# The first pass's down stage of a fused attention and gated-FFN block: one of seven products taken to a second level

## The chip, the cores and the metric

The kernel runs on one core of a Trainium2 chip. The metric is the device time of one execution in microseconds. Before the change the median of three runs is 753.28 us (752.81 to 753.76).

## What is computed

With 2048 tokens, D = 1024, 32 heads of 32 and F = 3584, all in bf16:

```
xn  = layernorm(x)
s   = linear_attention(xn, wqkv) @ wo        # phi(q) (phi(k)^T v) / (phi(q) sum phi(k))
ffn = (silu(xn @ w_gate) * (xn @ w_up)) @ w_down
out = x + s * silu(ffn)
```

The change concerns the last product, `@ w_down`, for the second half of the tokens, with the outer `silu`, the product with `s` and the addition of `x` that finish each result.

## The kernel before

The first 243 us or so make `s` and write it to DRAM (`s_dram`). What follows goes in two passes over 1024 tokens each; the one over tokens 1024 to 2047 comes first. A pass has 28 units (gate and up for 14 groups of 256 hidden columns) that fill `h`, and then the down stage, which multiplies `h` (1024 x 3584) with `w_down` (3584 x 1024). The first pass's down stage is `emit_down` (L1229), the last pass's `emit_down_m` (L1417).

All these products use a scheme with seven products in place of eight (Strassen's, in Winograd's form): both operands are cut in 2 x 2, seven products M1 to M7 of sums of the quarters are taken, and the four quarters of the result are C11 = M1 + M2, C12 = M1 + M6 + M5 + M3, C21 = M1 + M6 + M7 + M4 and C22 = M1 + M6 + M7 + M5. In the down stage the quarters of `h` are token halves of 512 by even and odd chunks of 128 hidden columns, those of `w_down` the matching rows by halves of 512 columns. The sums of weights are made once and kept in DRAM as tiles of two kinds: an "a" tile holds the weights of M1, M5, M6 and M7 for two steps of k, a "b" tile those of M2, M3 and M4 (seven tiles each).

`emit_down` works on four token tiles t = 0 to 3 of 128, each with 14 steps of k:

- **The a phase** (L1354): tiles 0 and 1, then 2 and 3, the second of each pair 6 steps behind (`LEAD`). `step_a` (L1253) issues four products of 512 columns per step: M1 into bank `dx`, M6 into `dy`, M7 and M5 into the double bank `dzw`. `evac_a` (L1281) copies M1 on ACT, adds on DVE, finishes C22's SiLU on ACT and keeps M1 and the sums.
- **The b phase** (L1382): first tiles 2 and 3, whose banks still hold M7, M5 and M1, then tiles 0 and 1 in fresh banks. `step_b` (L1272) issues three products of 512 columns: M2, M4 and M3. `evac_b` (L1303) adds what was kept (DVE) and takes the SiLUs (ACT).
- **Finishing a result** is `fin` (L1219): two DVE operations (times `s`, plus `x`), the output DMA on POOL's queue, and `io_load`, which loads the next `x` and `s` pair on SP's queue into one of five buffers, in the order of the list `fq`. A load waits until the output that last used its buffer has landed. The last three results of the pass are finished in the first three units of the next pass (`deferred`).
- **Work for the last pass**, which takes M1, M2, M4 and M7 each by seven products of a second level: `l2_early` (L1119) makes the second-level weight sums of M2 in free room of each b tile, four POOL operations per tile (L1137), and later stores them by three DMAs on SP (L1129 to L1131).
- **Sums for the next pass** (`emit_Ssum`, L706): four DVE operations of 128x2048, here between the two phases.

The orders of PE, DVE, ACT and POOL are the program's. SP's queue, which carries loads and stores, is ordered by a scheduler within `emit_down`; in most other parts by hand. Weight tiles rotate through eight slots: a b tile waits until the a tile in its slot has been read for the last time, and the next pass's tiles wait for the b tiles.

The second level in the last pass is `l2_M` (L1487). M is itself cut in 2 x 2 (256 tokens, 256 columns) and done by products 1, 2, 5, 6, 7, 4, 3, each two row tiles of seven matmuls of 256 columns (`l2_p`, L1473). Products share four banks: ACT copies half of a bank into another where two results share a sum (L1496, L1504), and between products 7 and 4 the banks are partly emptied by DVE while PE does other products (`fill`).

Of the kernel before, what the change touches and what calls it, by code (L numbers as in the profile page):

```python
# [21 lines left out]
def kernel(  # L22
# [11 lines left out]
    nc = tc.nc  # L34
# [919 lines left out]
    with ExitStack() as p3:  # L954
# [274 lines left out]
        def emit_down(p, h, base, last, more_S, next_S):  # L1229
# [13 lines left out]

            def alloc(t, phase):
                x_ = pps.tile([P, CW], FP32, name="dx", tag="s")
                y_ = pps.tile([P, CW], FP32, name="dy", tag="s") if phase == "a" else None
                zw = ppd.tile([P, 2, CW], FP32, name="dzw", tag="d")
                bk[t] = (x_, y_, zw)
# [3 lines left out]

            def step_a(t, k):  # L1253
                if k == 0:
                    alloc(t, "a")
# [8 lines left out]
            def prods_b(t, k, fresh):  # L1264
                x_, y_, zw = bk[t]
# [6 lines left out]
            def step_b(t, k, fresh):  # L1272
                if k == 0 and fresh:
                    alloc(t, "b")
                for f in prods_b(t, k, fresh):
                    f()

            fin_e = (nc.vector, nc.vector, nc.sync if last else nc.gpsimd)
            pend = []

            def evac_a(t, keep):  # L1281
# [5 lines left out]
                else:  # L1287
                    s1 = k2([P, CW], FP32, "s1")[:]
# [3 lines left out]
                nc.vector.tensor_tensor(out=s2, in0=y_[:], in1=s1, op=ALU.add)  # L1292
                nc.vector.tensor_tensor(out=s3, in0=zw[:, 0, :], in1=s2, op=ALU.add)
                c22 = k2([P, CW], FP32, "c22")[:] if keep else s3
                if keep:
                    nc.vector.tensor_tensor(out=u4, in0=zw[:, 1, :], in1=s2, op=ALU.add)
                nc.vector.tensor_tensor(out=c22, in0=zw[:, 1, :], in1=s3, op=ALU.add)
                g_ = k2([P, CW], BF16, "g22")[:]
                nc.scalar.activation(out=g_, in_=c22, func=ACT.Silu, scale=rch)
                pend.append(lambda: fin(p, t + TPB, 1, g_, *fin_e))  # L1300
                kept[t] = (s1, st[:, 1:3, :]) if keep else s2

            def evac_b(t, fresh):  # L1303
                x_, _, zw = bk[t]
                d = m4.tile([P, 2, CW], FP32, name="dd", tag="m4")
                g_ = k2([P, 2, CW], BF16, "g12")
                g11 = k2([P, CW], BF16, "g11")[:]
                if fresh:
                    s1, s34 = kept[t]
                    c11 = k2([P, CW], FP32, "c11")[:]  # L1310
                    nc.vector.tensor_tensor(out=d[:], in0=zw[:], in1=s34, op=ALU.add)
                    nc.vector.tensor_tensor(out=c11, in0=x_[:], in1=s1, op=ALU.add)
                    nc.scalar.activation(out=g_[:], in_=d[:], func=ACT.Silu, scale=rch)
                    nc.scalar.activation(out=g11, in_=c11, func=ACT.Silu, scale=rch)
                else:
                    s2 = kept[t]
                    nc.vector.tensor_tensor(out=d[:], in0=zw[:], in1=s2[:, None, :].to_broadcast([P, 2, CW]),
                                            op=ALU.add)
                    nc.scalar.activation(out=g11, in_=x_[:], func=ACT.Silu, scale=rch)
                    nc.scalar.activation(out=g_[:], in_=d[:], func=ACT.Silu, scale=rch)  # L1320
                return [lambda: fin(p, t + TPB, 0, g_[:, 0, :], *fin_e),
                        lambda: fin(p, t, 1, g_[:, 1, :], *fin_e),
                        lambda: fin(p, t, 0, g11, *fin_e)]

            def finish(t):
                ps = [ppd.tile([P, 2, CW], FP32, name="dz", tag="d")[:, 0, :]]
                ps += [pps.tile([P, CW], FP32, name="df%d" % i, tag="s")[:] for i in range(3)]
                s1, s34 = kept[t]
                t1, t2 = slice(t * P, (t + 1) * P), slice(TB + t * P, TB + (t + 1) * P)
                hs_ = [slice(0, 3 * CW // 4), slice(3 * CW // 4, CW)]  # L1330
                for i in range(2):
                    nc.scalar.copy(out=ps[2 + i][:, 0:hs_[i].stop - hs_[i].start], in_=s1[:, hs_[i]])
                for q, (r0, cc) in enumerate(((t + TPB, 0), (t, 1))):
                    for k in range(NFG):
                        lhs = h[:, 2 * k, t2].bitcast(F16) if q else h[:, 2 * k + 1, t2]
                        mm(ps[q], lhs, wb(k, 2 - q), k == 0, k == NFG - 1)
                    d = k2([P, CW], FP32, "d%d" % q)[:]
                    g_ = k2([P, CW], BF16, "g%d" % q)[:]
                    nc.vector.tensor_tensor(out=d, in0=ps[q], in1=s34[:, q, :], op=ALU.add)
                    nc.scalar.activation(out=g_, in_=d, func=ACT.Silu, scale=rch)  # L1340
                    if q == 0:
                        f0 = (r0, cc, g_)
                fin(p, *f0, *fin_e)
                fin(p, r0, cc, g_, *fin_e)
                g11 = k2([P, CW], BF16, "g11")[:]
                for i, cs in enumerate(hs_):
                    o_ = ps[2 + i][:, 0:cs.stop - cs.start]
                    for k in range(NFG):
                        mm(o_, h[:, 2 * k + 1, t1], wb(k, 0)[:, cs], False, k == NFG - 1)
                    nc.scalar.activation(out=g11[:, cs], in_=o_, func=ACT.Silu, scale=rch)  # L1350
                    fin(p, t, 0, g11, *fin_e, cols=cs)

            NS = NFG + LEAD
            for hf in range(2):  # L1354
                t0, t1 = 2 * hf, 2 * hf + 1
                for st in range(NS):
                    if st == 4:
                        while pend:
                            pend.pop(0)()
# [7 lines left out]
                    if st < NFG:  # L1367
                        step_a(t0, st)
                        if st == NFG - 1:
                            evac_a(t0, hf == 0)  # L1370
                    if st >= LEAD:
# [7 lines left out]
            if not last:  # L1379
                emit_rcl()  # L1380
                emit_Ssum(passes[passes.index(p) + 1])
            for hf in (1, 0):  # L1382
                t0, t1 = 2 * hf, 2 * hf + 1
                fresh = hf == 0
                endz = last and fresh
                for st in range(NFG if endz else NS):
                    if st == 4:
                        while pend:
                            pend.pop(0)()
                    if hf == 1 and not last and st % 2 == 1 and 2 in L2:  # L1390
                        if st // 2 < NQ:
                            l2_early(2, st // 2, False)
                        if 0 <= st // 2 - 2 < NQ:
                            l2_early(2, st // 2 - 2, True)
                    if st < NFG:
                        step_b(t0, st, fresh)
                        if st == NFG - 1:
                            fins = evac_b(t0, fresh)
                    if st >= LEAD and not endz:
                        step_b(t1, st - LEAD, fresh)  # L1400
                        if fresh and (st - LEAD) % 2 == 1:
                            load_w_to(base + 2 * NWA + (st - LEAD) // 2 + 2)
                if endz:
                    for f in fins:
                        f()
                    finish(t1)
                    break
                fins2 = evac_b(t1, fresh)
# [414 lines left out]
```

## Time and profile before

| | |
|---|---|
| median of the runs shown | 753.28 us |
| the profiled execution | 753.18 us |
| its span, first to last instruction | 751.4 us |
| PE, DVE, ACT, POOL busy | 744.1, 580.9, 383.0, 395.2 us |
| granted TensorE clock, whole span | 1.000 |
| a phase of the first pass | 413.86 to 462.20 us |
| b phase of the first pass | 462.20 to 498.46 us |
| units of the last pass | 498.46 to 668.00 us |
| last down stage | 668.00 to 751.40 us |

All times inside the execution are microseconds from the span's start. A matmul's own duration (379 ns for 512 columns) overlaps its neighbours'; what counts is the spacing of their starts.

### The profile page before, as it was taken

Reading aid. Unit: us, or ns where it says so; the run is one execution under the profiler, and the core shown is the slowest. Engines: PE = TensorE matmul, PEld = TensorE weight load, DVE = VectorE, ACT = ScalarE, POOL = GpSimd, SP = SyncE. Lnnn points to the kernel's source line nnn. Section 1 sums busy time; section 2 is a strip of 40 time slices with the busy share of each in tenths; the row PEclk is TensorE's granted clock in tenths of the full one; section 3 lists DMA queues with packets and bytes.
Section 4 is the critical chain, followed back from the end, with each engine's and each line's share of the span. In section 5 each row is a group of like instructions: output and inputs, shape, how many; then the busy total and the mean of one; then the engine's idle time right before and its main releaser. Section 6 shows DMA issues by size and latency. Waiting matters only on the chain.

```text
span 751.4 us, 11202 instructions
## 1 busy us (share of the span) xinstructions
PE 744.1 (99%) x3899; PEld 364.9 (49%) x3899; DVE 580.9 (77%) x1054; ACT 383.0 (51%) x549; POOL 395.2 (53%) x492
## 2 busy tenths in 40 slices
PE   8999999999999999999999999999999999999997
PEld 3544544454454444444444444444444444467664
DVE  6687787887697788888889894557777778688857
ACT  5677766889965666756558411132322232332023
POOL 2444799998540265858585021910767576940000
PEclk9999999999999999999999999999999999999999
DMA  9957799869688668888799418789989889478852
GB/s 316 302 145 147 217 335 304 307 146 261 218 203 281 222 225 295 291 310 291 283 304 404 157 42 296 227 261 373 327 302 321 315 285 363 161 224 315 275 187 98
DMA packets 132472, 194.20 MB, mean 258 GB/s; under 512 B 36432, under 2 KB 106192, under 8 KB 122688
## 3 DMA queue, kind: packets, MB, share of 16 engines
q1 hardware_dynamic: 124224, 159.21, 65.7%
q0 software_dynamic: 6752, 31.79, 11.0%
q10 hardware_dynamic: 1440, 2.49, 1.0%
q8 instruction: 30, 0.49, 0.3%
q14 instruction: 26, 0.21, 0.1%
HBM read 122.68 MB, written 63.44 MB: 248 GB/s over the span
## 4 chain that ended last, share of the span: by engine, by line
PE 96%; DVE 2%; ACT 1%; DMA 0%; issue 0%; ACTq 0%; DVEq 0%
PE zw L968 26%; PE kv_ps L556 15%; PE xb L968 13%; PE yb L968 7%; PE q_ps L183 6%; PE dzw L1251 6%; PE dm L1484 6%; PE dm L1448 5%; PE dx L1251 3%; PE fx L818 3%; PE s_ps L776 3%; PE dy L1251 2%; PE kvz L578 1%; PE nd L745 1%; DVE w_sb L311 0%; PE fx L776 0%
## 5 line engine op out<-in xcount | busy, mean ns | idle before, releaser
L968 PEld LDWEIGHTS <-w_sb 128*128 128x128 f16 (+1 forms) x1568 | 152.1, 98 | 182.9 <-DMA w_sb<-pk_u 0.5
L968 PE MATMUL xb<-xnT,w_sb 128*128 128x512 bf16 x448 | 115.0, 379 | 0.0
L556 PE MATMUL kv_ps<-wkv_sb,xnT 128*128 128x512 bf16 x512 | 113.7, 379 | 0.6 <-ACT xnT L545 0.4
L968 PE MATMUL zw<-xnT,w_sb 128*128 128x512 bf16 x448 | 105.8, 379 | 0.0
L968 PE MATMUL zw<-S,w_sb 128*128 128x512 f16 x448 | 105.8, 379 | 0.0
L323 POOL TENSOR_TENSOR w_sb<-w_sb 128x512 f16<-128x512 bf16 x42 | 50.2, 1196 | 95.7 <-DVE w_sb L311 51.3
L288 ACT ACTIVATE w_sb<-w_sb 128x2048 bf16<-128x2048 bf16 x42 | 79.9, 1902 | 4.4 <-DMA w_sb<-in_B_w_up_dram 4.4
L556 PEld LDWEIGHTS <-xnT 128*128 128x128 bf16 x512 | 48.3, 98 | 55.9 <-ACT xnT L545 0.8
L1149 POOL TENSOR_TENSOR w_sb<-w_sb 128x512 f16<-128x512 f16 (+3 forms) x48 | 52.7, 1118 | 29.1 <-DMA w_sb<-wd 28.2
L1044 ACT ACTIVATE sg<-cg 128x1024 bf16<-128x1024 f32 x28 | 29.6, 1057 | 57.4 <-DVE cg L1037 57.4
L183 PE MATMUL q_ps<-xnT,wq_sb 128*128 128x512 bf16 x256 | 58.4, 379 | 0.0
L968 PE MATMUL yb<-S,w_sb 128*128 128x512 f16 x224 | 57.4, 379 | 0.0
L1037 DVE SCALAR_TENSOR_TENSOR cg<-zw,rc_all,s 128x1024 f32<-128x1024 f32 x28 | 35.9, 1284 | 24.5 <-PE zw L968 12.5
L996 DVE SCALAR_TENSOR_TENSOR s<-yb,rc_all,s 128x512 f32<-128x512 f32 x42 | 31.4, 749 | 27.3 <-ACT s L995 27.3
L324 POOL TENSOR_TENSOR w_sb<-w_sb 128x512 f16<-128x512 bf16 x42 | 50.4, 1201 | 3.3
L326 POOL TENSOR_TENSOR w_sb<-w_sb 128x512 f16<-128x512 bf16 x42 | 50.3, 1197 | 0.0
L325 POOL TENSOR_TENSOR w_sb<-w_sb 128x512 f16<-128x512 bf16 x42 | 50.2, 1196 | 0.0
L1225 POOL DMA_DIRECT2D out_dram<-io x16 | 8.7, 544 | 74.5 <-DVE io L1224 74.2
L995 ACT ACTIVATE s<-xb,rcl 128x512 f32<-128x512 f32 x14 | 9.6, 687 | 65.4 <-PE xb L968 65.4
L1251 PE MATMUL dx<-w_sb,hT 128*128 128x512 bf16 x112 | 42.4, 379 | 0.0
L995 ACT ACTIVATE s<-xb,rc_all 128x512 f32<-128x512 f32 x42 | 28.3, 674 | 21.8 <-issue 12.8
L311 DVE TENSOR_SCALAR w_sb<-w_sb,cs_all 128x2048 bf16<-128x2048 bf16 x35 | 36.7, 1048 | 2.8
(221 smaller groups left out, 1334.6 us busy)
## 6 DMA issues: line engine op xcount, KB each, us to landing
w_sb<-pk_g SPq DMA_DIRECT2D x27, 1024.0 KB, 7.3
pk_g<-w_sb SPq DMA_DIRECT2D x14, 1024.0 KB, 5.1
w_sb<-pk_u SPq DMA_DIRECT2D x14, 1024.0 KB, 7.5
pk_u<-w_sb POOLq DMA_DIRECT2D x13, 1024.0 KB, 5.5
w_sb<-l SPq DMA_DIRECT2D x12, 896.0 KB, 4.7
l<-w_sb POOLq DMA_DIRECT2D x9, 896.0 KB, 8.0
w_sb<-in_B_w_gate_dram SPq DMA_DIRECT2D x14, 512.0 KB, 6.5
w_sb<-in_B_w_down_dram SPq DMA_DIRECT2D x28, 256.0 KB, 4.5
```

What stands on the lines that cost most here:

```text
L183: nc.tensor.matmul(q_ps[:], lhsT=wq_sb[:, dc, g * P:(g + 1) * P], rhs=xn_ap(dc, btok), start=(dc == 0), stop=(dc == DC - 1))
L288: nc.scalar.activation(out=junk, in_=raw_view(key, t), func=ACT.Square, accum_out=asum[:])
L323: nc.gpsimd.tensor_tensor(out=T1, in0=b12, in1=b11, op=ALU.subtract)
L324: nc.gpsimd.tensor_tensor(out=T2, in0=b22, in1=T1, op=ALU.subtract)
L325: nc.gpsimd.tensor_tensor(out=T3, in0=b22, in1=b12, op=ALU.subtract)
L326: nc.gpsimd.tensor_tensor(out=T4, in0=b21, in1=T2, op=ALU.subtract)
L556: mm = nc.tensor.matmul(kv_ps[:], lhsT=xn_ap(dc, tok), rhs=wkv_sb[:, dc, c * CW:(c + 1) * CW], start=(dc == 0), stop=(dc == DC - 1))
L968: mm = nc.tensor.matmul(out, lhsT=lhs(k), rhs=rhs(k), start=(first and k == 0), stop=(k == HK - 1), skip_group_check=True)
L995: nc.scalar.activation(out=s1[:], in_=x_[:], func=ACT.Copy, scale=rc)
L1149: nc.gpsimd.tensor_tensor(out=b(o_), in0=b(a_), in1=b(b_), op=ALU.subtract)
L1251: nc.tensor.matmul(out, lhsT=lhs, rhs=rhs, start=first, stop=lastk, skip_group_check=True)
L1484: nc.tensor.matmul(out, lhsT=lhs, rhs=w[:, j], start=i == 1 and j == 0, stop=j == NQ - 1, skip_group_check=True)
```

## The change

M2 of the first pass goes to the second level. The weight sums that it needs are those which `l2_early` makes anyway; they are now used from the b tiles as well as stored.

- `step_b` issues M4 and M3 alone. M2 becomes `l2_M2`: 98 products of 256 columns for all four tiles together, between the b phases of tiles 2 and 3 and of tiles 0 and 1. Its `fill` is the first four steps of tiles 0 and 1, which are now 2 steps apart (`LB`).
- Four new sums of quarters of `h` on DVE, 128x1792 each: `lhs12` behind tile 2's `evac_a`, `lhs34` behind tile 3's.
- POOL's weight sums for the second level are issued in the a phase, as the b tiles come, and no longer in the b phase; their stores stand on SP before the b phase (tiles 0 to 3) and behind it (4 to 6).
- `emit_Ssum` moves from before the b phase to behind `l2_M2`.
- In `l2_M2` the copies from bank to bank are issued ahead of tile 3's SiLU (in `evac_b`).
- SP's queue in `emit_down` is ordered by hand: all b loads and the next pass's first weight tile ahead of the stores; the other next weight tiles ahead of the last `x`/`s` loads (`hold`).
- The order of results changes. C11 of all tiles comes from `l2_M2`; the last four (C21 and C12 of tiles 0 and 1) are finished in the next pass, one behind its first unit, one behind the third and two behind the fourth. Their SiLUs lie in the fourth quarter of the `kept` tiles.

```diff
-            for hf in (1, 0):
-                for t in (2 * hf, 2 * hf + 1):
-                    fq += [(p, t + TPB, 0), (p, t, 1), (p, t, 0)]
+            fq += [(p, t + dt, cc) for t in (2, 3) for dt, cc in ((TPB, 0), (0, 1))]
+            fq += [(p, t, 0) for t in (1, 0, 3, 2)]
+            fq += [(p, t + dt, cc) for t in (0, 1) for dt, cc in ((TPB, 0), (0, 1))]
...
+            sp_man.enter_context(tc.manual_schedule(engines={mybir.EngineType.SP}))
...
-                return [lambda: mm(x_[:], h[:, 2 * k + 1, t * P:(t + 1) * P], wb(k, 0), f, l),
-                        lambda: mm(zw[:, 0, :], h[:, 2 * k + 1, t2], wb(k, 2), f, l),
-                        lambda: mm(zw[:, 1, :], h[:, 2 * k, t2].bitcast(F16), wb(k, 1), f, l)]
+                mm(zw[:, 0, :], h[:, 2 * k + 1, t2], wb(k, 2), f, l)
+                mm(zw[:, 1, :], h[:, 2 * k, t2].bitcast(F16), wb(k, 1), f, l)
...
+            def lhs12():
+                tt(l2_buf(5, 1), a21, a22)
+                tt(l2_buf(6, 2), sb[5], a11, ALU.subtract)
+
+            def lhs34():
+                tt(l2_buf(7, 0), a11, a21, ALU.subtract)
+                sb[3] = a21.bitcast(F16)
+                tt(sb[3], a12, sb[6], ALU.subtract)
...
+            def l2_M2(fill):
...
+                for r in range(2):
+                    l2_p(1, r, bank[r])
+                for r in range(2):
+                    nc.scalar.copy(out=bank[r][1][:, hi], in_=bank[r][0][:, lo])
+                evac_b(TPB - 1)
+                for r in range(2):
+                    l2_p(2, r, bank[r])
+                for r in range(2):
+                    l2_p(5, r, bank[r])
+                    l2_p(6, r, bank[r])
+                    nc.scalar.copy(out=bank[r][1][:, lo], in_=bank[r][1][:, hi])
+                flush()
+                for r in range(2):
+                    l2_p(7, r, bank[r])
+                cs = [m4.tile([P, 2, CW], FP32, name="dc", tag="m4") for r in range(2)]
+                for r in range(2):
+                    (xw, zy), c = bank[r], cs[r]
+                    tt(c[:, 1, hi], zy[:, lo], K[r][1][:, hi])
+                    tt(c[:, 0, hi], zy[:, hi], K[r][0][:, hi])
+                    tt(c[:, 0, lo], xw[:, lo], K[r][0][:, lo])
+                    tt(c[:, 1, hi], xw[:, hi], c[:, 1, hi])
+                fill()
+                for r in range(2):
+                    l2_p(4, r, bank[r])
+                for r in range(2):
+                    (xw, zy), c = bank[r], cs[r]
+                    tt(c[:, 1, lo], zy[:, lo], K[r][1][:, lo])
+                    fins.append((2 * r + 1, 0, silu(c[:, 1], "g11")))
+                    l2_p(3, r, bank[r])
+                    tt(c[:, 0, hi], xw[:, hi], c[:, 0, hi])
+                    fins.append((2 * r, 0, silu(c[:, 0], "g11")))
...
                         if hf == 1 and (st - LEAD) % 2 == 1:
                             load_w_to(base + NWA + (st - LEAD) // 2 + 2)
+                            l2_early(2, (st - LEAD) // 2, False)
...
+            lhs34()
+            emit_rcl()
+            for j in range(NQ - 3):
+                l2_early(2, j, True)
+            for st in range(NS):
+                if st < NFG:
+                    step_b(TPB - 2, st, False)
+                    if st == NFG - 1:
+                        flush()
+                        evac_b(TPB - 2)
+                if st >= LEAD:
+                    step_b(TPB - 1, st - LEAD, False)
+            for j in range(NQ - 3, NQ):
+                l2_early(2, j, True)
...
+            def b0(st):
+                if st < NFG:
+                    step_b(0, st, True)
+                if st >= LB:
+                    step_b(1, st - LB, True)
+                if st == NFG - 1:
+                    flush(2)
+                    evac_b0(0)
+                    flush(1)
...
+            l2_M2(fill)
+            emit_Ssum(passes[passes.index(p) + 1])
+            hold[0] = -1
+            for st in range(FB, NFG + LB):
+                load_w_to(base + 2 * NWA + (st - LB) // 2 + 1)
+                b0(st)
+            load_w_to(base + 3 * NWA + 1)
+            evac_b0(1)
+            hold[0] = False
+            flush(1)
+            while io_due:
+                io_due.popleft()
+                io_load()
+            deferred.extend([lambda: flush(1), lambda: None, lambda: flush(1), flush])
```

`flush(n)` finishes the next n waiting results (all without n) by `fin`, in the order in which their SiLUs were issued.

More of the change, by code (lines that the diff above doesn't have):

```diff
@@ L1227, in fin, with emit_down @@
                 io_load()
-        def emit_down(p, h, base, last, more_S, next_S):
+        def emit_down(p, h, base, more_S, next_S):
             def wa(k, q):
@@ L1242, in emit_down, with tt @@
             kept = {}
[L1244 to L1248, printed above, removed]
+            sp_man = ExitStack()
+            sp_man.enter_context(tc.manual_schedule(engines={mybir.EngineType.SP}))
             def mm(out, lhs, rhs, first, lastk):
                 nc.tensor.matmul(out, lhsT=lhs, rhs=rhs, start=first, stop=lastk, skip_group_check=True)
+            def tt(out, a, b_, op=ALU.add):
+                nc.vector.tensor_tensor(out=out, in0=a, in1=b_, op=op)
             def step_a(t, k):
                 if k == 0:
-                    alloc(t, "a")
+                    bk[t] = [pps.tile([P, CW], FP32, name=nm, tag="s") for nm in ("dx", "dy")]
+                    bk[t].append(ppd.tile([P, 2, CW], FP32, name="dzw", tag="d"))
                 x_, y_, zw = bk[t]
@@ L1262, in step_a, with step_b, flush, silu @@
                 mm(zw[:, 1, :], S1, wa(k, 0), f, l)
-            def prods_b(t, k, fresh):
-                x_, y_, zw = bk[t]
+            def step_b(t, k, fresh):
+                if k == 0 and fresh:
+                    bk[t] = [ppd.tile([P, 2, CW], FP32, name="dzw", tag="d")]
+                zw = bk[t][-1]
                 f, l = fresh and k == 0, k == NFG - 1
                 t2 = slice(TB + t * P, TB + (t + 1) * P)
-                return [lambda: mm(x_[:], h[:, 2 * k + 1, t * P:(t + 1) * P], wb(k, 0), f, l),
-                        lambda: mm(zw[:, 0, :], h[:, 2 * k + 1, t2], wb(k, 2), f, l),
-                        lambda: mm(zw[:, 1, :], h[:, 2 * k, t2].bitcast(F16), wb(k, 1), f, l)]
[L1272 to L1279, printed above, removed]
+                mm(zw[:, 0, :], h[:, 2 * k + 1, t2], wb(k, 2), f, l)
+                mm(zw[:, 1, :], h[:, 2 * k, t2].bitcast(F16), wb(k, 1), f, l)
+            fins = deque()
+            def flush(n=99):
+                while fins and n:
+                    fin(p, *fins.popleft(), nc.vector, nc.vector, nc.gpsimd)
+                    n -= 1
+            def silu(c, nm):
+                g_ = k2([P, CW], BF16, nm)[:]
+                nc.scalar.activation(out=g_, in_=c, func=ACT.Silu, scale=rch)
+                return g_
             def evac_a(t, keep):
@@ L1291, in evac_a @@
                 nc.scalar.copy(out=s1, in_=x_[:])
[L1292 to L1293 removed]
+                tt(s2, y_[:], s1)
+                tt(s3, zw[:, 0, :], s2)
                 c22 = k2([P, CW], FP32, "c22")[:] if keep else s3
                 if keep:
[L1296 to L1297 removed]
@@ L1298, in evac_a @@
[L1298 to L1304, printed above, removed]
-                d = m4.tile([P, 2, CW], FP32, name="dd", tag="m4")
[L1306 to L1351, printed above, removed]
@@ new lines, in evac_a, with evac_b @@
+                    tt(u4, zw[:, 1, :], s2)
+                tt(c22, zw[:, 1, :], s3)
+                fins.append((t + TPB, 1, silu(c22, "g22")))
+                kept[t] = (s1, st[:, 1:3, :] if keep else s2[:, None, :].to_broadcast([P, 2, CW]))
+            def evac_b(t, g_=None):
+                d = m4.tile([P, 2, CW], FP32, name="dd", tag="m4")
+                g_ = g_ or k2([P, 2, CW], BF16, "g12")
+                tt(d[:], bk[t][-1][:], kept[t][1])
+                nc.scalar.activation(out=g_[:], in_=d[:], func=ACT.Silu, scale=rch)
+                fins.extend([(t + TPB, 0, g_[:, 0, :]), (t, 1, g_[:, 1, :])])
@@ new lines, in emit_down, with l2_buf @@
+            A = quads(h, 1, 0)
+            aq = [A[:, k].rearrange("p j (r t n) -> p j r t n", r=2, t=2) for k in range(2)]
+            a11, a12, a21, a22 = aq[0][:, :, :, 0], aq[1][:, :, :, 0], aq[0][:, :, :, 1], aq[1][:, :, :, 1]
+            sb = {}
+            def l2_buf(i, s):
+                t = sp.tile([P, HK, TB], F16, name="S%d" % s, tag="S%d" % s)
+                sb[i] = t[:].rearrange("p a b -> p (a b)")[:, 0:2 * NQ * P].rearrange("p (j r n) -> p j r n", j=NQ, r=2)
+                return sb[i]
@@ new lines, in lhs12, with l2_p @@
+            def lhs12():
[5 more added lines that the diff above has]
+                tt(sb[3], a12, sb[6], ALU.subtract)
+            def l2_p(i, r, bank):
+                half, y0 = {1: (0, 0), 2: (0, 0), 5: (0, 1), 3: (0, 1), 6: (1, 1), 7: (1, 0), 4: (1, 0)}[i]
+                out = bank[half][:, y0 * CH:(y0 + 1) * CH]
+                lhs = {1: a11, 2: a12, 4: a22}.get(i)
+                lhs = sb[i] if lhs is None else lhs
+                for j in range(NQ):
+                    w = w_tiles[(p, "b", j)][:].rearrange("p h a b -> p (h a b)")
+                    if i <= 3:
+                        k, c = {1: (0, 0), 2: (1, 0), 3: (1, 1)}[i]
+                        w = w[:, 0:6 * CW].rearrange("p (k q c n) -> p q k c n", k=2, q=3, c=2)[:, M_PACK[2][1], k, c]
+                    else:
+                        w = w[:, 6 * CW:8 * CW].rearrange("p (b n) -> p b n", b=4)[:, (5, 6, 7, 4).index(i)].bitcast(F16)
+                    mm(out, lhs[:, j, r], w, i == 1 and j == 0, j == NQ - 1)
@@ new lines, in l2_M2 @@
+            def l2_M2(fill):
+                lo, hi = slice(0, CH), slice(CH, CW)
+                bank = [[pps.tile([P, CW], FP32, name="dm", tag="s")[:] for _ in range(2)] for r in range(2)]
+                K = [[kept[2 * r + i][0] for i in range(2)] for r in range(2)]
+                for r in range(2):
[29 more added lines that the diff above has]
+                    fins.append((2 * r, 0, silu(c[:, 0], "g11")))
@@ L1370, in emit_down @@
                             evac_a(t0, hf == 0)
+                            if hf == 1:
+                                lhs12()
                     if st >= LEAD:
@@ L1378, in emit_down @@
             load_w_to(base + 2 * NWA + 1)
[L1379 to L1408, printed above, removed]
-                for f in fins:
-                    f()
-                if fresh:
-                    deferred.extend(fins2)
-                else:
-                    for f in fins2:
-                        f()
@@ new lines, in emit_down, with evac_b0, fill @@
+            LB, FB = 2, 4
+            def evac_b0(t):
+                g_ = x_spare[t][:, 3, :].bitcast(BF16).rearrange("p (q n) -> p q n", q=2)
+                evac_b(t, g_)
+            def b0(st):
[7 more added lines that the diff above has]
+                    flush(1)
+            def fill():
+                for st in range(FB):
+                    b0(st)
```

9 lines of the change are left out of this document (5 added, 4 removed).

## The prediction

> **What bounds the kernel now.** I read the engines' busy times, then the stage itself as two windows, the chain that ended last, and the timelines of DVE, POOL and the DMA queues around it.
>
> ```profile
> PE 744.1 (99%) x3899; PEld 364.9 (49%) x3899; DVE 580.9 (77%) x1054; ACT 383.0 (51%) x549; POOL 395.2 (53%) x492
> ```
> ```profile
> 413.86:462.20 48.34, 48.34 (x225) 21.91 (x224) 34.23 (x71) 11.93 (x11) 6.74 (x10) 1.00 0.37 124
> 462.20:498.46 36.26, 36.26 (x169) 16.43 (x168) 19.26 (x28) 6.29 (x8) 17.86 (x28) 1.00 0.80 268
> 498.46:668.00 169.54, 169.54 (x787) 76.79 (x786) 129.22 (x152) 52.16 (x72) 98.38 (x115) 1.00 0.83 296
> ```
>
> The columns of the second fence are length, then busy time (and count) of PE, weight load, DVE, ACT and POOL, granted clock, DMA share and GB/s. The first-pass down stage runs from 413.86 to 498.46 us; in both halves PE is busy for the whole window. 392 products in 84.60 us are 0.2159 us each. So only less PE work can shorten the stage, and any new wait costs its full length.
>
> **What the change removes and adds on PE.** Removed: M2's 4 x 14 = 56 products of 512 columns, 56 x 0.2159 = 12.09 us. Added: 7 x 2 x 7 = 98 products of 256 columns. The last pass has such products already; the chain gives their rate, and one place where they waited:
>
> ```profile
> 668.00 18.34 PE dm L1484 x168
> ...
> 724.30 0.70 DVE c L1436
> ...
> 725.03 0.72 ACT g L1470
> 725.75 0.28 ACT dm L1496
> ...
> 726.07 6.27 PE dm L1484 x56
> ```
>
> 168 in 18.34 us are 0.1092 each, so 98 x 0.1092 = 10.70 us. Balance: -1.39 us. The lines from 724.30 show a bank-to-bank copy (L1496) behind a SiLU (L1470): PE stood from 724.28 to 726.07. In the new M2 the first copies precede the SiLU of tile 3, so that 1.8 us is not charged; in the 168 products at 668 the copies hid behind the next products as they do here.
>
> **A second gain.** The next pass's second weight tile now lands late:
>
> ```profile
> PEld L968 <- DMA w_sb<-pk_u: 0.5, 1, 0.5
> ```
> ```profile
> 502.08 1.02 PE yb L968 x4
> ```
>
> Four products take 0.86 elsewhere in this chain, so 0.16 us were lost. The tile was issued at 495.05, behind x/s loads on SP. In the change it waits for the end of M2 (487.6, below) and, on SP, for nine stores and four pairs of x/s loads that I place at 480 to 488. Issued at about 488 and landing in the 7.0 us seen, it is there at 495; it is needed at 500.5. I credit -0.16.
>
> **PE's new timetable** (old start 462.20). M4 and M3 of tiles 2 and 3: 56 x 0.2159, to 474.29. M2: products 1 and 2 to 477.35; 5 and 6 to 480.40; 7 to 481.93; twelve products of tiles 0 and 1 as filling, 2.59, to 484.52; products 4 and 3 to 487.58; the other 44 to 497.08. Against it I hold each engine.
>
> *The b tiles.* Fewer products make them due earlier: the last one at 470.0, not 473.9. In the old run it was issued at 462.2, behind stores, and took 9.5 us, to 471.7: 1.7 us late for the new timetable. But the new SP order puts all b loads ahead of the stores; each waits only for its a tile, the last for 460.5. With 6.9 us (the median) it lands at 467.4, with 9.5 at 470.0. Cost nothing; the cover left is 0 to 2.6 us.
>
> *DVE before M2.* Four sums of 128x1792 are new. From 128x512 in 0.417 us and 128x2048 in 1.22 comes 1.09 each (128x896 took 0.614). Two stand between the evacuations of tiles 2 and 3, ending at 458.54 and starting at 462.37 when ACT has copied; 2.2 us fit in 3.8, even with 0.4 us per operation of contention. Tile 3's first M4 product, at 465.2 instead of 466.5, needs the evacuation's last read, 464.6. Free, with 0.6 us left.
>
> *POOL, the tight engine.* Five of the seven sets of weight sums move from 471.9-485.9 to directly behind the second set, which begins at 456.48, when its b tile lands. The queue's next items are the output DMAs of C22 of tiles 2 and 3, at 470.55 and 471.35 in the old run. Undisturbed, one set takes 2.67 us, 24 operations 16.0. But DVE's sums disturb POOL, and the reverse:
>
> ```profile
> 656.35 0.67 POOL L1183 TENSOR_TENSOR kept<-hT,kept 128x256 f16<-128x256 bf16 x1
> ```
> ```profile
> 669.46 1.45 POOL L1183 TENSOR_TENSOR w_sb<-hT,w_sb 128x256 f16<-128x256 bf16 x1
> ```
> ```profile
> 482.86 0.88 DVE L1223 TENSOR_TENSOR g<-g,io 128x512 bf16<-128x512 bf16 x1
> ...
> 486.09 0.41 DVE L1223 TENSOR_TENSOR g<-g,io 128x512 bf16<-128x512 bf16 x1
> ```
>
> The 1.45 stands beside a DVE operation of 0.96, the 0.88 beside POOL's sums, the 0.41 after them. So a long DVE sum costs POOL about 0.8, a short one 0.1 (eight POOL operations in 6.09 us beside five), and POOL costs DVE 0.4. Four long and four short: +3.6, and POOL ends at 476.1. M2's product 5 needs the last set's first sum, about 474, at 478.0: free.
>
> *The wait that decides.* Behind POOL's run: C22's output of tile 2 must land before SP can load x and s for C12 of tile 3 (the eighth load in a rotation of five buffers; the stores ahead of it on SP are by then issued). The result is finished on DVE just ahead of the eight additions that empty M2's banks. If DVE waits there, products 4 and 3 wait. The DMA issues, quiet and loaded:
>
> ```profile
> out_dram<-io POOLq DMA_DIRECT2D x2, 128.0 KB, 2.0
> ```
> ```profile
> out_dram<-io POOLq DMA_DIRECT2D x2, 128.0 KB, 5.4
> ```
>
> Those are windows 443-446 and 470-472.5. At 476 the b tiles, the next first tile and four sets of stores have landed, and the other stores wait on SP behind this load, so I take 2.0. Then 0.4 to issue, 2.6 to land, 0.9 for two DVE operations: the additions can start at 482.1. PE needs the fifth of them (four went in 1.32 in the last pass, 686.71 to 688.03 from start to start) by 485.28, so they may start up to 483.47. Slack 1.4 us; beyond it the stall is one to one.
>
> *The rest.* The next pass's S sums (4 x 1.22 us) move from 464.6 to about 488-493, needed from 497.1: free, 4 us left. Four results rather than three are finished in the next pass, two in its fourth unit (0.85 us more DVE there); DVE has 40 us idle in that pass's 169.5, so free, 0.85 if not. Their SiLUs lie in spare buffers, so no other result waits for them; their x/s loads go behind seven weight loads, but the first use is a unit later.
>
> **Sum.** -1.39 - 0.16 = -1.55 us. The profiled execution took 753.18 (span 751.4 and 1.78 around it); it becomes 751.63. It lies 0.10 below the median of 753.28, so I forecast 751.7.
>
> [...] By the rows, the two engines overlap in part while they disturb each other. [...]
>
> **Rivals.**
> [...]
> 2. *Slower: loaded landings on the same chain.* The output lands in 5.4 as at 470 and the load in 4.4 as at 488.5-491; from 476.1, with 0.4 and 0.9, DVE starts at 487.2 and PE waits 3.7: 755.4. It decides wherever landing and load together exceed the quiet 4.6 by 1.4. For it: DMA share was 0.80 in this half. Against: much of that traffic is moved out of the way. The output's 5.4 alone gives 485.5, a wait of 2.0, 753.7.
> 3. *Slower: the next weights come late.* My 488 has SP send a store every 0.42 us; in the old run pairs came at 468.11, 470.00 and 471.86, 0.94 per store. Nine such move the tile's issue to 492.7; with 7.0 us to land it is still in time (500.5), with the 12.3 that the first tile took it is 4.5 late: 756.2. Against: both would have to hold.
> 4. *It does not do what it says*: if the small products, here on b tiles in another layout, ran no better than 0.1234 each, the saving would be nil: 753.1. 168 of 168 at 0.1092 speak against it.
>
> **How the numbers follow.** Forecast 751.7 has 0.58; rival 1 with the partial cases 0.20; rival 2 0.14; rival 3 0.04; rival 4 0.04. 0.2%, about what a measurement of this kernel can tell from no change, is 1.5 us: 751.8 and 754.8. The whole gain lies on that edge; of the forecast's 0.58 I put 0.40 below 751.8 and 0.18 above. Faster 0.40, same 0.42, slower 0.18. The range begins at 751.3 (another 0.1 us of small waits in the next pass, 169.54 against 784 x 0.2159 = 169.27, and 0.3 of spread between runs) and ends at 754.3, above the 753.7 of a single loaded landing; rivals 2 and 3 stay outside.
>
> **What would show it.** Right: PE busy throughout the stage, 98 products of 256 columns, the stage 83.2 us long, no wait for the next pass's second tile; DVE waiting for an x/s load before M2's additions, ending by about 482 counted from this trace; POOL's 24 sums ending near 476. Wrong: a PE wait named for DVE at products 4 or 3 (the decisive chain, and its length is the error), for DMA at a b tile, or at the first or second weight tile of the next pass; small products above 0.11 us.

## The result, and the profile after

The changed kernel takes 751.73 us (median of 16 runs, 751.26 to 751.84), the kernel before, run beside it, 753.35 (16 runs, 752.57 to 753.90): a ratio of 0.9978, 95% interval 0.9971 to 0.9986. It is faster by 1.6 us, just over the 0.2% that a measurement here can tell, and the interval reaches down to 0.14%. The forecast was 751.7.

The engines' busy times of the page, after:

```profile
PE 743.4 (99%) x3941; PEld 369.6 (49%) x3941; DVE 587.2 (78%) x1068; ACT 384.0 (51%) x553; POOL 398.2 (53%) x492
```

42 matmuls more, and 0.7 us less of PE's time: 1.4 less in the down stage, while the first 243 us, ahead of all that the change touches, happen to have 0.7 more in this execution (240.60 against 239.87). The span is 750.0 us instead of 751.4. The same three windows as before, cut where the a phase, the b phase and the next pass begin (length, PE, weight load, DVE, ACT, POOL, clock, DMA share, GB/s):

```profile
413.86:462.20 48.34, 48.34 (x226) 21.91 (x224) 36.69 (x73) 11.93 (x12) 11.35 (x16) 1.00 0.41 145
462.20:497.08 34.88, 34.88 (x212) 20.56 (x211) 25.20 (x41) 7.29 (x12) 15.69 (x23) 1.00 0.91 302
497.08:666.60 169.52, 169.52 (x788) 76.90 (x786) 127.34 (x152) 52.40 (x72) 98.92 (x115) 1.00 0.81 287
```

PE is busy for the whole of each. POOL's sums have moved forward, in part into the first window (11.35 us busy, 6.74 before), and the DMA share of the second rose from 0.80 to 0.91. The chain of work that ended last, through the b phase into the next pass (start, length, work):

```profile
462.05 12.52 PE dzw L1247 x58
474.57 7.64 PE dm L1247 x70
482.21 2.59 PE dzw L1247 x12
484.80 3.06 PE dm L1247 x28
487.86 9.50 PE dzw L1247 x44
497.35 0.86 PE yb L968 x4
...
500.81 0.86 PE yb L968 x4
```

Every piece begins where the one before it ended. The 98 small products (70 and 28) take 10.70 us, 0.1092 each. From the first product of the a phase (413.97 in this trace) to the first of the next pass (497.19 in PE's timeline) it is 83.22 us, where it was 84.60: **1.38 less**. The four products at 500.81 are those that waited for the second weight tile before; the next pass's units now take 169.38 us instead of 169.54: **0.16 less**. Together 1.54; the trace after started its a phase 0.11 later, so the span shows 1.4.

What the prediction called the tight engine, in POOL's timeline (start, length, line, shape, count, and in brackets the idle time before and what ended it):

```profile
452.95 2.66 POOL L1137 TENSOR_TENSOR w_sb<-w_sb 128x256 f16<-128x256 bf16 x4 [4.73 <-DMA w_sb<-wd]
456.31 2.67 POOL L1137 TENSOR_TENSOR w_sb<-w_sb 128x256 f16<-128x256 bf16 x4 [0.70 <-DMA w_sb<-wd]
460.10 13.76 POOL L1137 TENSOR_TENSOR w_sb<-w_sb 128x256 f16<-128x256 bf16 x16 [1.12 <-DMA w_sb<-wd]
473.80 1.09 POOL L1225 DMA_DIRECT2D out_dram<-io  x2
```

and on DVE, at the wait that was to decide:

```profile
479.51 0.43 DVE L1223 TENSOR_TENSOR g<-g,io 128x512 bf16<-128x512 bf16 x1 [1.04 <-DMA io<-s_dram]
...
481.55 0.75 DVE L1250 TENSOR_TENSOR dc<-dm,kept 128x256 f32<-128x256 f32 x2 [1.15 <-PE dm L1247]
```

POOL's run ended at 473.86 and not at 476.1. The decisive `x`/`s` load had landed by 479.5, DVE was free at 480.40, and then it was DVE that waited for PE's product 7, not PE for DVE.

### The profile page after: what moved, and what is told of

It reads as the page before. It is cut to its first block, busy times and chain, and to the rows that moved or that the text cites. A ratio compares the mean times of both kernels' runs of the same rounds, so it can differ in the third digit from the quotient of the medians.

```text
span 750.0 us, 11301 instructions
## 1 busy us (share of the span) xinstructions
PE 743.4 (99%) x3941; PEld 369.6 (49%) x3941; DVE 587.2 (78%) x1068; ACT 384.0 (51%) x553; POOL 398.2 (53%) x492
## 4 chain that ended last, share of the span: by engine, by line
PE 96%; DVE 3%; ACT 1%; issue 0%; DVEq 0%; ACTq 0%
PE zw L968 26%; PE kv_ps L556 15%; PE xb L968 13%; PE yb L968 6%; PE q_ps L183 6%; PE dzw L1247 6%; PE dm L1526 6%; PE dm L1490 5%; PE s_ps L776 3%; PE fx L818 2%; PE dy L1247 2%; PE dx L1247 2%; PE dm L1247 1%; PE kvz L578 1%; PE nd L745 1%; PE warm_ps L592 1%
## 5 line engine op out<-in xcount | busy, mean ns | idle before, releaser
L996 DVE SCALAR_TENSOR_TENSOR s<-yb,rc_all,s 128x512 f32<-128x512 f32 x42 | 31.4, 749 | 29.3 <-ACT s L995 29.3
L183 PEld LDWEIGHTS <-wq_sb 128*128 128x128 bf16 x256 | 24.4, 98 | 27.5
```

The source lines that it names most:

```text
L183: nc.tensor.matmul(q_ps[:], lhsT=wq_sb[:, dc, g * P:(g + 1) * P], rhs=xn_ap(dc, btok), start=(dc == 0), stop=(dc == DC - 1))
```

## The experiments

All kernels start from the changed one. The kernel before took 753.24 to 753.34 us beside them; ratios are to it.

### 1. Where the gain is: M2 at the first level, all else kept

The body of `l2_M2` is replaced by the 56 products of 512 columns, in the same place and with the same filling; the last of the four sums of quarters of `h`, which only product 3 reads and which would overwrite what the 56 products read, is left out.

```diff
-                for r in range(2):
-                    l2_p(1, r, bank[r])
-...
+                for t in range(TPB):
+                    for k in range(NFG):
+                        mm(bank[t // 2][t % 2], h[:, 2 * k + 1, t * P:(t + 1) * P], wb(k, 0), k == 0, k == NFG - 1)
+...
+                for t in (1, 0, 3, 2):
+                    tt(c, bank[t // 2][t % 2], K[t // 2][t % 2])
```

> The changed kernel with M2 alone put back to 56 products of 512 columns, at the place where the 98 small ones stand (all of M2, then the filling steps, then four additions of 512 columns); every other move of the change is kept, only the last of the four sums of quarters of h, which would overwrite what M2 reads, is left out. My theory, that the gain is PE's product time and nothing else but 0.16 us: 12.09 in place of 10.70 us, so 1.39 slower than the changed kernel, 753.1 us, with PE busy through the stage, 84.6 us long. Rival, that the gain comes from the moves (queue order, copies, deferred results): about 751.7.

Measured: 752.97 us (752.70 to 753.22, 10 runs), ratio 0.9994 [0.9984, 1.0004]. Its chain in the same place:

```profile
474.61 12.09 PE dm L1247 x56
486.69 12.09 PE dzw L1247 x56
...
502.23 0.86 PE yb L968 x4
```

12.09 us for M2 where the second level has 10.70. The stage ends 1.43 us later than in the changed kernel and is 84.61 us long (414.01 to 498.62 in PE's timeline), as in the kernel before; and the second weight tile (502.23) is in time here too. So nearly all of the gain is the second level's arithmetic, not the reordering around it.

### 2. The copies behind the SiLU

```diff
-                for r in range(2):
-                    nc.scalar.copy(out=bank[r][1][:, hi], in_=bank[r][0][:, lo])
                 evac_b(TPB - 1)
+                for r in range(2):
+                    nc.scalar.copy(out=bank[r][1][:, hi], in_=bank[r][0][:, lo])
```

> The changed kernel with tile 3's addition and SiLU issued ahead of the first two copies from bank to bank. Theory: product 2 overwrites the columns that the copy reads, so it waits for the copy; in the changed kernel the first copy ends at 475.78 and product 2 starts at 475.93. Behind the SiLU (its input is ready at 475.84, it takes 1.15) the copy ends at about 477.4: PE waits 1.5 us, 753.2 us. Rival, taken from the one place of the last pass where such a copy stands behind a SiLU and PE waits 0.3 us: 752.0 or less.

Measured: 753.09 us (752.84 to 753.43), ratio 0.9993 [0.9981, 1.0004]. Its PE timeline:

```profile
474.27 1.69 PE L1247 MATMUL dm<-w_sb,hT 128*128 128x256 bf16 x14
477.20 1.69 PE L1247 MATMUL dm<-w_sb,hT 128*128 128x256 bf16 x14 [1.24 <-ACT dm L1353]
```

ACT's SiLU of 1.15 us stands ahead of the copies, and PE waits 1.24 us for the first of them. The bracket counts from the end of the matmul before, which would have overlapped its successor by 0.16 (a matmul of 256 columns takes 272 ns in this stage, with starts 0.1092 us apart). From start to start, product 1 takes 2.93 us here (474.27 to 477.20) where 14 x 0.1092 = 1.53 is usual: 1.40 more. So the whole gain of M2's second level hangs on this order of two lines. In the changed kernel the copies begin at 475.42 and 476.13, beside the 28 products of 1 and 2, and the SiLU at 476.40.

### 3. SP's order left to the scheduler

```diff
-            sp_man = ExitStack()
-            sp_man.enter_context(tc.manual_schedule(engines={mybir.EngineType.SP}))
...
-            sp_man.close()
```

> The changed kernel with SP's queue in this stage left to the scheduler, which puts the stores of the first three b tiles between the b loads again, but the last b load and the next pass's first tile still ahead of the rest. Theory: a b load that is issued by about 460.5 and lands in up to 9.5 us is in time (470.0), so nothing changes: 751.7 us. Rival, that the order by hand is what saves the earlier deadlines of the b tiles: PE waits up to 1.7 us for the last one, 753.4.

Measured: 753.21 us (752.90 to 756.36), ratio 1.0001 [0.9991, 1.0011]. My theory, that the order costs nothing, falls; the rival holds, with three late tiles and not one. SP's queue, PE and PE's weight loads:

```profile
460.29 1.52 SPq L249 DMA_DIRECT2D w_sb<-wd  x3
```
```profile
467.42 2.89 PE L1244 MATMUL dzw<-w_sb,hT 128*128 128x512 f16 x12 [0.95 <-DMA w_sb<-wd]
```
```profile
467.42 1.60 PEld L1244 LDWEIGHTS <-hT 128*128 128x128 f16 x8 [1.24 <-issue]
469.29 1.60 PEld L1244 LDWEIGHTS <-hT 128*128 128x128 f16 x8 [0.26 <-issue]
471.16 4.85 PEld L1244 LDWEIGHTS <-hT 128*128 128x128 f16 x25 [0.27 <-issue]
```

What SP itself waited for between 449 and 461 us (in all, times, longest):

```profile
SPq L1129 <- DMA w_sb<-wd: 4.0, 1, 4.0
SPq L1131 <- POOL w_sb L1137: 1.9, 1, 1.9
```

The stores for the last pass (L1129 to L1131, the last ahead of these loads at 459.75) stand ahead of the b loads on SP. One waits 4.0 us for the b tile that it stores from, one 1.9 us for POOL's sums, and the loads wait behind them. The last three b tiles go out from 460.29 on and take 7.1, 8.4 and 9.7 us: they land at 467.4, 469.2 and 471.1, each just ahead of the first product that reads it. PE loses 1.12 us at the first, from start to start. At the other two the profile names no releaser, but each stretch of eight products between 467.42, 469.29 and 471.16 takes 1.87 us where 8 x 0.2159 = 1.73 is usual, 0.14 more. Together it is 1.4, and so much longer is the stage (413.63 to 498.26, 84.6 us). The medians differ by 1.5. The spans differ by only 1.0 (751.0 against 750.0), because this execution began its a phase 0.34 us earlier. In the changed kernel the six loads are one run from 447.69 to 461.10.

### 4. The last four results finished at once

```diff
-            deferred.extend([lambda: flush(1), lambda: None, lambda: flush(1), flush])
+            flush()
```

> The changed kernel with the last four results finished at the end of the stage, ahead of the next pass's first unit, in place of in its units. Theory: their x/s loads are issued at 500 to 502 behind the next weights and land some 3 to 5 us later, DVE is held until about 506 and then needs 3.4 us more; the first unit's banks are emptied late, at about 514 in place of 508.4, so PE waits 3 to 6 us: 755 to 757 us. Rival, that results finished on DVE lie off the path: 751.7.

Measured: 766.69 us (766.03 to 767.13), ratio 1.0178 [1.0163, 1.0193]. The direction was right and the size far too small. DVE and PE:

```profile
514.08 0.42 DVE L1223 TENSOR_TENSOR kept<-kept,io 128x512 bf16<-128x512 bf16 x1 [13.32 <-DMA io<-s_dram]
```
```profile
518.90 3.33 PE L968 MATMUL zw<-xnT,w_sb 128*128 128x512 bf16 x8 [13.86 <-DVE s L1010]
```

The first of these `x`/`s` pairs is issued from 500.64 on, behind seven weight loads of 1 MB, and lands only at 514, 13.0 us later. DVE is idle for 13.32 us until then, does the first unit's evacuation behind it (L996 to L1010, 516.47 to 518.85), and PE waits 13.86 us for that. On top, the eight products at 518.90 take 3.17 us from start to start (1.73 usual). 13.86 + 1.44 = 15.3; the span is longer by 15.4.

### 5. How much slack POOL has: four or ten more sums

N operations of POOL's kind (128x256, rewriting one sum with the same value) behind the last set, ahead of the outputs:

```diff
+            for _ in range(N):
+                nc.gpsimd.tensor_tensor(out=Tj[:, 3].bitcast(F16), in0=rj[:, 1, 0], in1=Tj[:, 1].bitcast(F16), op=ALU.subtract)
             load_w_to(base + 2 * NWA + 1)
             lhs34()
```

> The changed kernel with four more POOL operations ahead of the outputs (the last weight sum of the last b tile repeated, 0.67 us each, same result). Theory with the slack that the trace of the changed kernel shows: the chain POOL, output, x/s load, DVE ends at 480.4 and may end at 483.6, so 2.7 us more still cost nothing, 751.7 us. Rival, the slack of 1.4 us that was worked out blind: PE waits 1.3, 753.0.

> The same with ten more POOL operations, 6.7 us. Theory: the chain ends at 487.1, 3.5 us beyond what PE can bear, and PE waits for DVE between the filling and product 4: 755.2 us. Rival, that this chain lies beside PE's work whatever its length: 751.7.

Measured: with four 751.95 us (751.65 to 752.40), ratio 0.9979 [0.9970, 0.9988]; with ten 758.49 (758.25 to 759.30), ratio 1.0069 [1.0054, 1.0084]. DVE with four:

```profile
482.65 0.42 DVE L1223 TENSOR_TENSOR g<-g,io 128x512 bf16<-128x512 bf16 x1 [4.07 <-DMA io<-s_dram]
...
483.45 1.08 DVE L1250 TENSOR_TENSOR dc<-dm,kept 128x256 f32<-128x256 f32 x3
```

DVE now waits 4.07 us for the load, and the additions start at 483.45. Products 4 and 3 in the changed kernel, then with four more operations:

```profile
484.64 3.22 PE L1247 MATMUL dm<-w_sb,hT 128*128 128x256 f16 x28
```
```profile
484.56 3.47 PE L1247 MATMUL dm<-w_sb,hT 128*128 128x256 f16 x28
```

They take 0.25 us longer: the second row tile of product 4 starts at 485.57 and not 0.11 after the matmul at 485.21. The sixth addition ends at 485.52, so this is what it seems to wait for; the profile names no releaser for so short a gap. The medians differ by 0.22. With ten, POOL, DVE and PE:

```profile
473.98 7.76 POOL L1412 TENSOR_TENSOR w_sb<-w_sb 128x256 f16<-128x256 bf16 x10
481.68 2.68 POOL L1225 DMA_DIRECT2D out_dram<-io  x5
```
```profile
487.47 0.42 DVE L1223 TENSOR_TENSOR g<-g,io 128x512 bf16<-128x512 bf16 x1 [7.01 <-DMA io<-s_dram]
```
```profile
489.08 5.40 PE L1247 MATMUL dm<-w_sb,hT 128*128 128x256 f16 x28 [4.48 <-DVE dc L1250]
```

The chain that the prediction named exists: POOL, output, load, DVE, PE. The additions start at 488.28 (DVE's timeline), and PE restarts at 489.08, behind the second of them (it ends at 489.02). By the 4.48 us of this wait the limit for product 4's first row tile is 483.8. The second row tile's limit comes first: put beside the changed kernel, where it starts at 485.40, the run with four has it at 485.40 - (485.57 - 483.45) = 483.3. The prediction had 483.47. With DVE free at 480.40 the changed kernel's slack is 2.9 us, not 1.4. Of the 3.3 us beyond what I expected, 1.1 is that an operation took 0.78 beside DVE and not 0.67, and 2.2 that the 28 products behind the wait take 5.23 us, start to start, instead of 3.05.

### 6. The next pass's weights later: two tries

First the loads at the end of the program's loop instead of inside it:

```diff
             for st in range(FB, NFG + LB):
-                load_w_to(base + 2 * NWA + (st - LB) // 2 + 1)
                 b0(st)
             load_w_to(base + 3 * NWA + 1)
```

> The changed kernel with the next pass's second to eighth weight tile issued when the stage ends and not as the b tiles come free. Theory: the second tile is issued at about 497.3 in place of 489.2, lands in the 6.9 us that it took, at 504.2, and is needed at 500.6: PE waits 3.6 us, 755.3 us; up to 760 if the seven tiles share the queues so that it takes the 11.8 us that is their median. A rival that calls the weight order free would stay at 751.7.

Measured: 751.68 us (751.33 to 751.99, 9 runs), ratio 0.9977 [0.9968, 0.9987]. It tested nothing: between these lines nothing else goes to SP, so SP's queue is the same; the next pass begins at 497.3 (497.2 in the changed kernel) and both spans are 750.0, so the loads' place among PE's instructions made no difference here. It serves as a repeat of the changed kernel. Then behind the last four `x`/`s` pairs, which undoes that part of the change:

```diff
-                load_w_to(base + 2 * NWA + (st - LB) // 2 + 1)
                 b0(st)
-            load_w_to(base + 3 * NWA + 1)
             evac_b0(1)
...
             while io_due:
                 io_due.popleft()
                 io_load()
+            load_w_to(base + 3 * NWA + 1)
```

> One ordering of the change undone: the next pass's weight tiles (all but the first) are loaded behind the last four x/s pairs on SP and no longer ahead of them; nothing else changes. Theory (my third rival's mechanism, priced from the changed kernel's trace): those pairs wait for buffers whose outputs are issued as the results of 493.5 to 500.0 are finished, the last of them at about 500.1; with 2.0 to 2.8 to land, the last pair is issued at about 502.6 and the second weight tile at 503.4; with the 6.9 it takes alone it lands at 510.3. PE needs it at 500.6, so it waits 9.7 us (more if the transfer shares the queues: 11.9 is the median there), and the matmuls behind the idle run at a lower granted clock, as the 28 products behind a 4.5 us wait did in another run (5.2 instead of 3.06 us), so 2 to 5 more. About 764.5, between 761 and 768. Later weight tiles come every 1.7 us and are used every 3.4, so no further wait. Rival: the pairs' buffers are free early (the pairs ahead of them were sent at 484.7 to 489.1 without a stall) and the tile goes out by 494: then nothing changes, 751.7.

Measured: 762.53 us (762.44 to 763.04), ratio 1.0123 [1.0105, 1.0141]. SP's queue and PE:

```profile
502.40 0.33 SPq L1214 DMA_DIRECT2D io<-in_A_x_dram  x1
...
503.30 0.38 SPq L265 DMA_DIRECT2D w_sb<-pk_u  x1
```
```profile
508.51 1.89 PE L968 MATMUL yb<-S,w_sb 128*128 128x512 f16 x4 [7.86 <-DMA w_sb<-pk_u]
...
514.88 1.03 PE L968 MATMUL xb<-xnT,w_sb 128*128 128x512 bf16 x4
```

The last pair went out at 502.40 (expected 502.6), the tile at 503.30 (503.4); it landed in 5.2 us and not 6.9. The wait is 7.86, and the 16 products from 508.51 to 514.88 take 6.37 us instead of 3.45 (16 x 0.2159): 2.92 more. 7.86 + 2.92 = 10.8, the difference of the spans.

### 7. The same lesson in the last pass

The prediction read a stall of 1.8 us into the last pass's M4, where a copy stands behind a SiLU. Here that SiLU, of the last C22 tile, is issued behind the copies:

```diff
+                if mid is not None:
+                    mid()
                 for r in range(2):
                     l2_p(M, 2, r, A, bk)
...
-                fins.append((t + TPB, 1, silu(c, "g22")))
+                if t < TPB - 1:
+                    fins.append((t + TPB, 1, silu(c, "g22")))
...
+                    mid=lambda: fins.append((TPB + TPB - 1, 1, silu(c, "g22")))))
```

> The changed kernel with the same order, copies ahead of the SiLU, also in the last pass, at its M4 (the SiLU of the last tile of C22 is issued behind the two copies). The trace shows one PE wait there, 0.3 us for a copy. Theory: it goes, 751.4 us, 0.3 less than the changed kernel. Rival, that my reading of the chain there (1.8 us on DVE, ACT and copy) is a wait of PE: 749.9 us; or that the next wait takes its place: 751.7.

Measured: 751.25 us (750.88 to 751.64), ratio 0.9969 [0.9958, 0.9981], the fastest of all kernels here. The chain there has products 1, 2, 5, 6 and 7 of M4 in one piece now, where it had gone through DVE and ACT:

```profile
722.80 7.64 PE dm L1526 x70
```

70 x 0.1092 = 7.64: no wait is left in it. The gain is PE's wait in the waits view of the kernel before, 0.3 us there and 0.44 from start to start (product 1 takes 1.97 us instead of 1.53), and not 1.8. The spans differ by 0.5 and the medians by 0.48 (751.25 against 751.73), though the ranges of the runs overlap.

## Why the prediction was right, point by point

- **PE's balance, -1.39.** 1.38 measured; the small products ran at 0.1092 on the b tiles too. Rival 4 is out, and experiment 1 puts the gain here.
- **The second weight tile, -0.16.** Measured 0.16. The tile went out at 489.22 and not 488, and landed in 6.9 us, by 496.1, against a need at 500.8. Experiment 6 shows that this order carries weight: behind the last pairs the tile costs 10.8 us. My rival 3 (4.5 late, 756.2) did not come: the issue was 3.5 us ahead of the 492.7 that it took, and the landing took 6.9 and not 12.3. Its price also left out the products that run slowly behind a wait (2.92 us in experiment 6).
- **"PE stood from 724.28 to 726.07": wrong.** The chain follows one path backwards; that its steps there are DVE and ACT does not mean that PE was idle. PE did the 14 matmuls of product 1 from 724.10 and stood for 0.28 us (0.44 from start to start) before the 14 of product 2, as its own timeline of the kernel before has it:

```profile
724.10 1.69 PE L1484 MATMUL dm<-w_sb,hT 128*128 128x256 f16 x14
726.07 1.69 PE L1484 MATMUL dm<-w_sb,hT 128*128 128x256 f16 x14 [0.28 <-ACT dm L1496]
```

 The 1.8 did not enter the sum. The conclusion drawn from it, that the copies must come first in the new M2, holds by experiment 2, at 1.40 us.
- **The b tiles, cost nothing.** Right; and the reason given, loads ahead of stores, is what keeps it so (experiment 3: 1.4 us lost without it). The last tile went out at 460.79, took 7.8 us and landed at 468.6, 1.5 ahead of its first product; the cover forecast was 0 to 2.6.
- **DVE's four sums, free.** They took 1.36, 1.09, 1.29 and 1.44, within the 0.4 allowed each; PE has no wait there.
- **POOL's end at 476.1: off by 2.2.** Its mis-sized term is the start. I began the run at 456.48, when the second b tile landed in the old trace. But that landing hung on the same SP order that I had credited for the last b tile: in the changed kernel the loads go out from 447.69 and POOL's second set begins at 452.95, 3.5 earlier. Of that, 1.8 went into waits for the next two b tiles (0.70 and 1.12). The contention was nearly right: 24 operations took 2.66 + 2.67 + 13.76 = 19.09 us, 3.1 over the undisturbed 16.0, where I had 3.6. So -3.5 + 1.8 - 0.5 = -2.2.
- **The slack.** Output and load took 5.7 us from 473.80 to 479.51, where I had 5.0. The limit was right to 0.2, though product 4 seems to wait for the sixth addition and not the fifth. Slack 2.9 and not 1.4, by experiment 5.
- **Rival 1, POOL standing still for the whole of DVE's sums (0.20 with the partial cases).** No run shows that: eight two-input operations of DVE, 6.0 us undisturbed, cost POOL 3.1. Some 1.1 us of DVE's sums lie in POOL's idle time before 460.10, and of the other 4.9 POOL lost 3.1. DVE lost 0.8 on the long sums and 1.2 on three of the short ones. In part, on both sides. The three f32 operations of `evac_a` from 456.44 to 458.66, each with one input in PSUM, fell beside POOL's set at 456.31, which took 2.67 us; the set at 452.95, with DVE idle, took 2.66.
- **Rival 2, loaded landings.** The landings were 0.7 longer than I took, not 5.2, though the DMA share was 0.91 in this half. Experiment 5 agrees with its price, about one to one beyond the limit, and adds the slow products to it.
- **S sums, deferred results.** S sums at 488.24 to 493.1 (forecast 488 to 493). The four deferred results cost nothing in the next pass; not deferring them costs 15 us.

The sum was right because both terms on PE's path were, and every cover held. POOL's early end was not foreseen, but the forecast did not need it: with the end at 476.1 there was still slack. The range's upper part stood for waits that did not come. The chance of "same" was large because the gain lies at the edge of what can be told, and there it came out.

## What to carry to other kernels

Where one engine was busy all the time, as PE in this stage, the gain was the change of that engine's work, by a rate read from the same instructions elsewhere in the trace (1.39 us worked out, 1.38 measured); all the other work is to show that each cover holds, and the covers here are worth 1 to 15 us each against a gain of 1.5. SP's order of loads and stores set the start of another engine too (POOL's second set began at 452.95 and not at 456.48): a new order must be carried through to every engine that waits for its loads, not only to the one that is in doubt. And the 1.8 us of DVE and ACT steps in the chain of the kernel before was not PE's idle time, which was 0.28 us: the waits view or PE's own timeline has that, and the spacing of starts has its full cost (1.40 where the bracket has 1.24).

## What the runs showed of the hardware

**Three waits of PE cost more than their length.** Experiments 6, 5 (ten more operations) and 4 had a wait of 7.86, 4.48 and 13.86 us, and paid 2.92, 2.2 and 1.44 us more in slow products. The granted clock is the third number from the right. Experiment 6 (stop at 500.65, restart at 508.51):

```profile
503.00:504.00 1.00, 0.00 (x0) 0.00 (x0) 0.27 (x1) 0.00 (x0) 0.00 (x0) 1.00 0.54 138
504.00:505.00 1.00, 0.00 (x0) 0.00 (x0) 0.00 (x0) 0.00 (x0) 0.00 (x0) 0.60 1.20 239
...
513.00:514.00 1.00, 1.00 (x3) 0.30 (x2) 0.67 (x1) 0.40 (x1) 0.00 (x0) 0.50 1.00 426
514.00:515.00 1.00, 1.00 (x5) 0.45 (x4) 0.00 (x0) 0.00 (x0) 0.00 (x0) 0.78 0.95 401
```

The clock fell to half at about 504.2 (0.60 is 0.2 us at full and 0.8 at half) and came back at 514.4. Worked out the same way, with ten more POOL operations (0.88 in 486 to 487, 0.71 in 493 to 494) it fell at 486.8 and came back at 493.6 (stop 484.59, restart 489.08), and without the deferral (0.60 in 508 to 509, 0.58 in 521 to 522) it fell at 508.2 and came back at 521.8 (stop 505.05, restart 518.90). So in these three it fell 3.6, 2.2 and 3.2 us after the stop and was back 5.9, 4.5 and 2.9 us after the restart. At half the clock half of that time is lost, by this estimate 2.9, 2.3 and 1.5 us, beside the 2.92, 2.2 and 1.44 measured. From fall to return it is 10.2, 6.8 and 13.6 us. The waits of 0.95 and 1.24 us (experiments 3 and 2) left the clock at 1.00 in the same view.

**Small loads behind large ones.** By the DMA issues, the `x` and `s` loads of 128 KB each, which took 2.2 and 2.5 us (medians) in the quieter stretch of experiment 6's last kernel, took 13.0 from issue to landing, the first pair, behind seven loads of 1 MB in experiment 4.
